# Moving loads between queues in a fused attention-and-FFN backward kernel: columns over GpSimd, a transposed operand in quarters, a written order for the output stage

## The chip, the core and the metric

The kernel is one launch on one core of a Trainium2 chip. A core has five instruction streams that run beside each other and meet at semaphores: TensorE (PE in the profile: matmuls out of SBUF into PSUM, with the weight loads PEld), VectorE (DVE), ScalarE (ACT), GpSimd (POOL) and SyncE (SP). Data moves between HBM and SBUF by DMAs, which one of SyncE, ScalarE and GpSimd issues from its own in-order stream; all of them share the core's 16 DMA engines. An instruction at the head of a stream that waits for a semaphore holds everything behind it in that stream, whether that is a DMA issue or a compute instruction.

The metric is the device time of the launch in microseconds. Before the change it is 803.75 us, the median of six runs between 796.22 and 813.41.

## What is computed

The reference is a block of linear attention and a SwiGLU FFN, each behind a LayerNorm and with a residual, on x of 2048 x 640 in bf16, and the gradients of its output with respect to x and the five weights, for a given grad_out:

```python
def _A_ref(x, wqkv, wo):                    # 32 heads of 20
    q, k, v = split(x @ wqkv)
    phi = lambda t: jnp.where(t > 0, t + 1, jnp.exp(t)) + 1e-6
    pq, pk = phi(q), phi(k)
    kv = jnp.einsum("bhsd,bhse->bhde", pk, v)
    z = jnp.einsum("bhsd->bhd", pk)
    num = jnp.einsum("bhqd,bhde->bhqe", pq, kv)
    den = jnp.einsum("bhqd,bhd->bhq", pq, z)[..., None] + 1e-6
    return merge_heads(num / den) @ wo
def _B_ref(x, w_gate, w_up, w_down):        # 640 -> 1728 -> 640
    return (_silu(x @ w_gate) * (x @ w_up)) @ w_down
h = x + _A_ref(_layernorm(x), A_wqkv, A_wo)
out = h + _B_ref(_layernorm(h), B_w_gate, B_w_up, B_w_down)
# returned: out, and the vjp of grad_out for x, wqkv, wo, w_gate, w_up, w_down
```

## The kernel before

The 2048 rows are 16 tiles of 128 rows (`ST = 16`), the 640 columns five blocks of 128 (`DT = 5`). PSUM holds four two-bank tiles at a time, all from one pool (`mm`). SBUF is parted into pools whose buffers are reused: five large ones, four "strips" (tag "S"), two pools of row tiles (`wk`), a ring of seven `fw` tiles, and three staging tiles "stg".

The stages in order of time: LayerNorm 1 with keys and queries (0 to 52 us); the attention forward; the FFN forward and its weight gradients in four groups `g` of 448, 448, 448 and 384 of the 1728 hidden columns (143 to 449 us); the gradient of the hidden activations, in eight pairs of row tiles (449 to about 570 us); the attention backward (to about 724 us); the output stage (to 800 us).

**The FFN groups.** For each group a loop over pairs of row tiles makes gate and up products (L796, L801), the activation on ScalarE (L817 to L823) and seven products on VectorE (L829). SyncE then transposes each tile of gradients by DMA into a staging tile and stores it to the scratch `scr_dT` (L832, L785). After the loop `dw_group` makes the group's weight gradients: plain products in `dw` (`ps_dw`, L881, copied out by `copy` at L883 on ScalarE or VectorE) alternate with a fast scheme of sums and products (`ps_wa`, `ps_wc`, L690; sums on VectorE, L686). In the last group (g = 3) VectorE also makes sums of the gate weights (`wg_tsum`, L658) and of the first columns (`col_sum`, L669).

**The columns.** The next stage reads the transposed gradients back in pairs of row tiles: `load_cols(p)` loads pair p from `scr_dT` in four DMAs, one for each group, into a strip. Pairs 0 and 1 are loaded on ScalarE's queue by `act_load`, which keeps the written order: pair 0 right before `dw_group` of group 3, pair 1 at its end. Pairs 2 to 7 go over GpSimd's queue (`pool_load`, where the scheduler picks the place). `pool_store` is a DMA on GpSimd's queue that keeps its written order against other such DMAs. On GpSimd's queue also stand the stores of all weight gradients, the loads `pq` for rows 13 to 15 (L641), which use the three staging tiles, and later the loads `pkr`.

[...]

**Around GT.** At the end of the backward pairs, `dp_1` and `dp_2` finish the gradient of the queries tile by tile: `dp_a` and `dp_b` on VectorE, two `widen` copies and the copies out of PSUM on ScalarE. TensorE meanwhile makes the five products `ps_gt` (L929), copied to `GT` by ScalarE (L1201 for the first, L1244 for the others). `xn_act` normalises rows of x on ScalarE, as filler for that stage. Then `xnT_r`, the transposed normalised x, is loaded in four quarters of 640 KB, all held until `last_pq`, the last load of `pq`, by `tc.issue_after`; SyncE at the same time transposes 16 pieces of `wqkv` (`wqkvT`), then pieces for `ring`, `wvk` and `ring` again. The loop that follows runs `t` over 19 steps: `ps_dk` of tile t (L110), and `ps_dxn` of tile t - 3 (L1364).

**The output stage.** out = h + FFN in seven pairs of row tiles by a fast scheme (`step_a` to `step_f`), with the tiles of h loaded over GpSimd's queue (`load_h1`, L1394) and most of the results stored there (`o_store`, L1479). `load_mT` is SyncE's transposing load of the hidden activations. TensorE and ScalarE keep the written order; GpSimd's order is the scheduler's.

Of the kernel before, what the change touches and what calls it, by code (L numbers as in the profile page):

```python
# [13 lines left out]
EngineType = mybir.EngineType  # L14
# [6 lines left out]
def kernel(  # L21
# [600 lines left out]
    with tc.manual_schedule(engines={EngineType.SP}):  # L622
# [48 lines left out]
        def dw_group(g, w, m_s, dd, dw, dwd_part, dgu_part):  # L671
# [95 lines left out]
            tt(ev[:, :, :w], pc[:, :, :w], u2, ALU.add)  # L767
            store(ev, 1, 0)
            if g == 3:
                load_cols(1, act_load)  # L770

        wgT = {}

# [13 lines left out]
        for g in range(4):  # L787
# [59 lines left out]
            if g == 0:  # L847
                wdT = strips.tile([P, DT, 2 * GM], BF16, name="wdT", tag="S")
                load_wdT(wdT, 2)
            elif g == 1:  # L850
                wgT[0] = big.tile([P, 16, D], BF16, name="wgT", tag="B")
                for gg in range(2):
                    tr_wgT(gg)
                    load_wgu(gg + 2)
            elif g == 2:
                dm_t[3] = strips.tile([P, ST, GM], BF16, name="dm3", tag="S")
                act_load(dm_t[3][:, :, :GW[3]], scr_dm_v)
                wgT[1] = big.tile([P, 16, D], BF16, name="wgT", tag="B")
                tr_wgT(2)
                tr_wgT(3)  # L860
            else:
                for c in range(4):
                    pool_store(scr_m_v[:, c * 4:(c + 1) * 4, F:FT * P], m_s[:, c * 4:(c + 1) * 4, w - 64:w])
                pool_store(mat_v(scr_dwdT)[:, 0:4, F:FT * P], zpad)
                pool_store(mat_v(scr_dwdT)[:, 4, F:FT * P], zpad[:, 0, :])
                load_cols(0, act_load)
                wsum = big.tile([P, ST * D], BF16, name="wsum", tag="B")
                for i in (1, 2):
                    wg_t[i] = wsum[:, (i - 1) * HKG * 320:i * HKG * 320].rearrange("p (k n) -> p k n", k=HKG)
                wg_t["S1"] = wsum[:, 2 * HKG * 320:2 * HKG * 320 + HKG * P].rearrange("p (k c) -> p k c", k=HKG)  # L870
# [61 lines left out]
    with tc.manual_schedule(engines={EngineType.PE, EngineType.DVE, EngineType.Activation, EngineType.SP, EngineType.Pool}):  # L932
# [49 lines left out]
        def load_q(t):  # L982
            if 0 <= t < ST:
                pqs[t] = small.tile([P, D], BF16, name="pq", tag="stg", bufs=3, padded_shape=[P, 7 * P])[:]
                return nc.gpsimd.dma_start(out=pqs[t], in_=scr_pq_v[:, t, :]).ins

        def dp_mm(t):
            if t >= 0:
# [178 lines left out]
        kb = [dqs[:, i * D:(i + 1) * D] for i in (8, 9, 10)]  # L1167
        prs, rxs = [kb[0], junk], kb[1:]

        def dp_1(t):  # L1170
            dp_a(t, prs[t % 2])
            widen(rxs[t % 2], rall, t)
            widen(prs[t % 2], nS1, t)

        def dp_2(t):
            last = dp_b(t, prs[t % 2], rxs[t % 2])
            return last, load_q(t + 3)

        dp_1(ST - 5)
        dp_mm(ST - 4)  # L1180
# [3 lines left out]
            gts[i] = mm("ps_gt")  # L1184
            gt_part(gts[i], i, 0, ST - 4, ST if i else 4)
        dp_mm(ST - 3)
        dp_1(ST - 3)
        last_pq = dp_2(ST - 4)[1]
        nc.gpsimd.dma_start(out=hn[:, ST - 4:ST, :], in_=x_v[:, ST - 4:ST, :])
        store_dwd(p - 1)  # L1190
        store_dwd(p)
        gts[2] = mm("ps_gt")
        gt_part(gts[2], 2, 0, ST - 4)
        dp_mm(ST - 2)
        xn_act(range(6, 9))
        dp_1(ST - 2)
        dp_2(ST - 3)
        GT = mat(2 * DT * D, DT, D)
        ps = gts.pop(0)
        gt_part(ps, 0, ST - 4, ST)  # L1200
        nc.scalar.copy(out=half(GT[:, 0, :]), in_=row(ps))  # L1201
        dp_mm(ST - 1)
        xn_act(range(9, 11))
        dp_1(ST - 1)
        dp_2(ST - 2)
        xn_act(range(11, ST - 4))
        last_dq = dp_2(ST - 1)[0]

    with tc.manual_schedule(engines={EngineType.SP, EngineType.DVE}):

# [18 lines left out]
        for k in (0, 1):  # L1229
            for i in range(DT):  # L1230
                with tc.issue_after(last_dh1T):
                    tr_piece(wqkvT[:, 5 * k:5 * k + 5, :], A_wqkv[:, k * D:(k + 1) * D], i)
        for c in range(4):
          with tc.issue_after(last_pq):
            pool_load(xnT_r[:, 4 * c:4 * c + 4], scr_xnT[4 * c:4 * c + 4].rearrange("t p k c -> p t k c"))

        for i in range(1, DT):
            ps = gts.pop(i, None)
# [81 lines left out]
        def load_mT(t):  # L1320
            if t % 4 == 0:
                mTs[t // 4] = strips.tile([P, 4, FT, P], BF16, name="mT", tag="S")
            nc.sync.dma_start_transpose(out=mTs[t // 4][:, t % 4], in_=scr_m[t * P:(t + 1) * P, :])

        for t in range(ST + LAG):
            if t in (2, 3):
                dwqk(0, t + 1)
            if t < ST:
                if t + 2 < ST:
                    load_pk(t + 2)  # L1330
                pkr = pkrs.pop(t)
                nc.vector.tensor_scalar(out=pkr[:], in0=pkr[:], scalar1=-1e-6, scalar2=1.0, op0=ALU.add, op1=ALU.min)
                tk = wk("tk", pool=1)
                ps = mm("ps_dk")
                mm_row(ps, lambda i: xnT_r[:, t, i, :], lambda i, n0, n1: WK2[:, i, n0:n1], DT)
                nc.vector.scalar_tensor_tensor(out=half(tk[:]), in0=row(ps), scalar=rstd1[:, t:t + 1] if t < NC else 1.0,
                                               in1=half(dzb[:]), op0=ALU.mult, op1=ALU.add)
                nc.vector.tensor_tensor(out=dk[:, t, :], in0=tk[:], in1=pkr[:], op=ALU.mult)
                nc.sync.dma_start_transpose(out=ring[:, t % 4], in_=dk[:, t, :])
                if t < 2:  # L1340
                    load_pqT(t + 1)
            if 8 <= t < 8 + HG:
                tr_cols(G[:, t - 8, :], scr_GT, OH[t - 8])
            if t == 14:
                nc.sync.dma_start_transpose(out=KV.rearrange("p j c -> p (j c)").unsqueeze(1), in_=scr_KVT)
            if t == ST:
                dKV = stage()[:, :HG, :]
                nc.sync.dma_start_transpose(out=dKV, in_=dKVT.rearrange("p j c -> p (j c)"))
            if t == ST:
                wd = big.tile([P, FT, D], BF16, name="wd", tag="B")  # L1350
                nc.sync.dma_start(out=wd[:, :13, :], in_=B_w_down[0:13 * P, :].rearrange("(j p) d -> p j d", p=P))
                for r in (0, 64):
                    nc.sync.dma_start(out=wd[r:r + 64, 13, :], in_=B_w_down[13 * P:F, :])
            u = t - LAG
            if u < 0:
                continue
            if t >= ST:
                dwqk(1, t - ST)
            pkT, dqT, dkT = ring[:, 4 + u % 3], ring[:, 7 + u % 3], ring[:, u % 4]
            ps = mm("ps_dxn")  # L1360
            for ci, (n0, n1) in enumerate(NCH):
                for k, (lhs, rhs) in enumerate(((dqT, wqkvT[:, 0:5]), (pkT, WV2), (dkT, wqkvT[:, 5:10]))):
                    for i in range(DT):
                        nc.tensor.matmul(ps[:, ci, :320], lhsT=lhs[:, i, :], rhs=rhs[:, i, n0:n1],  # L1364
                                         start=(k == 0 and i == 0), stop=(k == 2 and i == DT - 1))
            if u + 3 < ST:
                load_pqT(u + 3)
            if ST - MTA <= u:
                load_mT(u - ST + MTA)
            dx = wk("dx")  # L1370
            ln_bwd(ps, xn_r[:, u, :], rstd1[:, u:u + 1], dh1[:, u, :], dx[:], 0)
            nc.gpsimd.dma_start(out=o1_v[:, u, :], in_=dx[:])
# [10 lines left out]
        def dwv(i):  # L1383
# [2 lines left out]
            mm_heads(ps, lambda j: Y[:, j, i * P:(i + 1) * P], lambda j, a, b: dKV[:, j, a:b])  # L1386
            nc.scalar.copy(out=half(ev[:]), in_=row(ps))
            nc.sync.dma_start(out=out_2[i * P:(i + 1) * P, 2 * D:3 * D], in_=ev[:])

        h1rs = {}  # L1390

        def load_h1(t):
            h1rs[t] = wk("h1r", pool=t % 2)
            nc.gpsimd.dma_start(out=h1rs[t][:], in_=scr_h1_v[:, t, :])  # L1394

        NP = ST // 2 - 1
        HK = 6
# [97 lines left out]

        CH15 = [(0, 320), (320, 512), (512, 640)]

        with tc.manual_schedule(engines={EngineType.PE, EngineType.Activation}):
            for t in range(4):
                load_h1(t)  # L1500
            for t in (5, 6):
                load_mT(t)
# [16 lines left out]

            for p in range(NP):  # L1520
                v = p - 1
                load_h1(2 * p + 4) if 2 * p + 4 < ST else None
                load_h1(2 * p + 5) if 2 * p + 5 < ST else None
                for t in (2 * p + 7, 2 * p + 8):
                    if t < ST:
                        load_mT(t)
                for j in range(2 * p + 2, min(2 * p + 4, HG)):
                    tr_cols(Y[:, j, :], scr_Yt, OH[j])
                step_a(p)
                if v < 0:  # L1530
                    tt(T4, B21, T2)
                    next(fill)
                    step_b(p)
                    step_c(p)
                    osum(p + 1, 0)
                    osum(p + 1, 1)
                    next(fill)
                    next(fill)
                    tt(T5, BL[0], BL[1])
                    for k, i in ((0, 3), (1, 2), (1, 3)):  # L1540
                        osum(p + k, i)
                    continue
                step_d(v)
                step_b(p)
                c22(v)
                osum(p + 1, 0)
                step_c(p)
                step_e(v)
                osum(p + 1, 2)
                step_f(v)  # L1550
                osum(p + 1, 1)
                osum(p + 1, 3)
                if p not in (2, 3):
                    f, i = small_q.pop(0)
                    f(i)
# [63 lines left out]
```

## Time and profile before

The profiled execution took 801.75 us, of which 800.0 us are the span from its first to its last instruction.

| what | measured |
|---|---|
| median of six runs | 803.75 us |
| profiled execution, and its span | 801.75 us, 800.0 us |
| TensorE busy | 782.0 us, 98% of the span |
| VectorE, ScalarE, GpSimd busy | 72%, 41%, 28% |
| mean granted TensorE clock | 0.994 of full speed |
| PE busy in 410 to 430 us | 12.27 of 20 us, clock 0.83 |
| PE busy in 735 to 769 us, and 769 to 800 us | 32.05 of 34, and 26.56 of 31 us |
| column loads issued by ScalarE (8): issue of one; landing | 0.37 to 0.50 us; median 5.1 us |
| column loads issued by GpSimd (24): issue of one; landing | 0.71 to 0.73 us; median 5.2 us |

A line of the timeline gives start and length in us, the engine (with q: its DMA queue), the line of the source, the operation and its tiles, the number of instructions, and in brackets how long the engine was idle before and what ended it. A line of the waits names who waited for whom, the total, the number of times and the longest. Matmul ends in the timeline are modelled, so the pace of matmuls is read from start to start.

### The profile page before, as it was taken

What the parts mean: (1) busy time and instruction counts of PE and PEld (TensorE: products, weight loads), DVE (VectorE), ACT (ScalarE), POOL (GpSimd) and SP (SyncE); (2) the same over time, 40 slices, a digit from 0 to 9 for tenths busy, and PEclk for the clock granted to TensorE, in tenths of its full rate; (3) what the DMA queues carried; (4) which work ended last, traced back from release to release, by engine and by line L of the source; (5) the groups of instructions that cost most, each with busy time, mean ns of one, the idle gap of its engine ahead of it and who ended that gap; (6) DMA issues with size and microseconds to landing.
All of it is one profiled execution on the core that took longest, in us unless ns stands there. A gap on an engine that the chain in (4) does not pass through costs nothing.

```text
span 800.0 us, 13753 instructions
## 1 busy us (share of the span) xinstructions
PE 782.0 (98%) x5243; PEld 498.3 (62%) x5243; DVE 575.6 (72%) x1005; ACT 331.7 (41%) x490; POOL 221.3 (28%) x375
## 2 busy tenths in 40 slices
PE   9999999999999999999996999999999999999988
PEld 7676566555555555555653677777667677777655
DVE  7979988894697648747974777999882366626763
ACT  6972532760283145402810245676662133333001
POOL 4600047413301111144032253532431112114220
PEclk9999999999999999999997999999999999999999
DMA  9799999999979978999796789998999988899992
GB/s 259 157 240 307 197 225 251 262 266 235 225 187 225 216 172 202 251 252 229 175 211 190 202 245 232 186 231 200 191 223 205 162 173 169 174 256 245 189 237 75
DMA packets 295731, 170.62 MB, mean 213 GB/s; under 512 B 242780, under 2 KB 283741, under 8 KB 295664
## 3 DMA queue, kind: packets, MB, share of 16 engines
q1 hardware_dynamic: 271552, 102.84, 63.7%
q0 software_dynamic: 19584, 61.57, 27.8%
q10 hardware_dynamic: 4528, 5.33, 2.2%
q8 instruction: 41, 0.67, 0.4%
q14 instruction: 26, 0.21, 0.1%
HBM read 52.92 MB, written 56.28 MB: 136 GB/s over the span
## 4 chain that ended last, share of the span: by engine, by line
PE 84%; DVE 7%; DMA 5%; SPq 2%; issue 1%; ACT 1%; POOL 0%; ACTq 0%; DVEq 0%
PE ps_dw L881 9%; PE ps_dxn L1364 8%; PE ps_dhn L955 7%; PE ps_wa L690 7%; PE pg L796 6%; PE pu L801 6%; PE ps_dm L423 5%; PE ps_dhc L955 5%; PE ps_dwqk L1283 5%; PE ps_kq L311 4%; PE ps_wc L690 3%; PE ps_y L514 3%; PE ps_a L577 3%; PE ps_dk L110 2%; PE ps_oa L1434 2%; PE pdm L423 2%
## 5 line engine op out<-in xcount | busy, mean ns | idle before, releaser
L955 PEld LDWEIGHTS <-cols 128*128 128x128 bf16 x624 | 61.1, 98 | 23.7
L796 PE MATMUL pg<-wgu,hnT 128*128 128x448 bf16 (+1 forms) x320 | 63.6, 346 | 0.0
L801 PE MATMUL pu<-wgu,hnT 128*128 128x448 bf16 (+1 forms) x320 | 63.6, 346 | 0.0
L881 PE MATMUL ps_dw<-m_s,dh 128*128 128x448 bf16 (+1 forms) x320 | 60.7, 347 | 0.0
L1364 PEld LDWEIGHTS <-ring 128*128 128x128 bf16 x480 | 46.9, 98 | 19.6 <-DMA ring<-dk 1.5
L1364 PE MATMUL ps_dxn<-wqkvT,ring 128*128 128x320 bf16 x320 | 51.3, 299 | 1.2 <-DMA ring<-dk 1.2
L881 PEld LDWEIGHTS <-dh 128*128 128x128 bf16 x320 | 31.5, 98 | 27.5 <-issue 0.7
L801 PEld LDWEIGHTS <-hnT 128*128 128x128 bf16 x320 | 31.3, 98 | 27.1
L796 PEld LDWEIGHTS <-hnT 128*128 128x128 bf16 x320 | 31.3, 98 | 27.0
L423 PEld LDWEIGHTS <-dh2T 128*128 128x128 bf16 x320 | 31.0, 98 | 25.1
L423 PE MATMUL ps_dm<-wdT,dh2T 128*128 128x448 bf16 (+1 forms) x240 | 46.5, 344 | 0.0
L311 PE MATMUL ps_kq<-wqk,xnT 128*128 128x320 bf16 x320 | 45.3, 301 | 0.7 <-DMA xnT<-xn 0.7
L817 ACT ACTIVATE dd<-pg 128x896 bf16<-128x896 f32 (+1 forms) x32 | 28.5, 891 | 40.4 <-PE pg L796 36.0
L690 PEld LDWEIGHTS <-S 128*128 128x128 bf16 x256 | 25.7, 101 | 31.1 <-issue 10.4
L311 PEld LDWEIGHTS <-xnT 128*128 128x128 bf16 x320 | 31.1, 99 | 13.2 <-DMA xnT<-xn 1.0
L1283 PEld LDWEIGHTS <-hn 128*128 128x128 bf16 x320 | 31.0, 98 | 12.2 <-issue 0.3
L140 POOL TENSOR_SCALAR lnv<-mv 128x1 f32<-128x1 f32 x32 | 11.9, 373 | 90.8 <-DVE mv L136 73.9
L843 POOL DMA_DIRECT2D scr_m<-m_s x16 | 12.1, 757 | 88.7 <-DVE m_s L829 88.7
L148 DVE CUSTOM_DVE_ANT_0 lb_a<-lb_dy,hn 128x640 bf16<-128x640 bf16 x16 | 13.2, 825 | 31.7 <-ACT lb_dy L146 31.7
L690 PE MATMUL ps_wc<-dd,S 128*128 128x448 bf16 (+1 forms) x128 | 27.2, 370 | 7.7 <-ACT dwev L883 7.7
L686 DVE TENSOR_TENSOR dd<-dd 128x3584 bf16<-128x3584 bf16 (+1 forms) x12 | 23.1, 1953 | 13.4 <-PE ps_wa L690 13.4
L146 ACT ACTIVATE lb_dy<-ps_dxn,rstd 128x640 bf16<-128x640 f32 x16 | 12.7, 794 | 46.3 <-PE ps_dxn L1364 46.3
(259 smaller groups left out, 1781.5 us busy)
## 6 DMA issues: line engine op xcount, KB each, us to landing
scr_dT<-stg SPq DMA_DIRECT2D x48, 224.0 KB, 3.1
cols<-scr_dT POOLq DMA_DIRECT2D x18, 448.0 KB, 5.2
scr_m<-m_s POOLq DMA_DIRECT2D x12, 448.0 KB, 4.6
pq<-scr_pq POOLq DMA_DIRECT2D x32, 160.0 KB, 5.4
hn<-in_A_x_dram SPq DMA_DIRECT2D x5, 640.0 KB, 5.6
scr_dT<-stg SPq DMA_DIRECT2D x16, 192.0 KB, 3.1
cols<-scr_dT ACTq DMA_DIRECT2D x6, 448.0 KB, 5.1
scr_pq<-pqa SPq DMA_DIRECT2D x4, 640.0 KB, 4.7
```

Source lines behind the costliest of these rows:

```text
L311: nc.tensor.matmul(ps[:, ci, :320], lhsT=xnT[:, t, k, :], rhs=wqk[:, k, w0 + n0:w0 + n1], start=(k == 0), stop=(k == DT - 1))
L423: nc.tensor.matmul(ps[:, c, :w], lhsT=dh2T[:, kt, (t + c) * P:(t + c + 1) * P], rhs=wdT[:, kt, o:o + w], start=(kt == 0), stop=(kt == DT - 1))
L514: nc.tensor.matmul(ps[:, ci, :320], lhsT=xn[:, t, i * P:(i + 1) * P], rhs=pk[:, t, n0:n1], start=(t == 0), stop=(t == ST - 1))
L577: nc.tensor.matmul(ps[:, ci, :320], lhsT=pqsT[:, i, t * P:(t + 1) * P], rhs=W2[:, i, n0:n1], start=(i == 0), stop=(i == DT - 1))
L690: nc.tensor.matmul(out, lhsT=lhs[:, t, :], rhs=rhs[:, t, :], start=(first and t == 0), stop=(t == 7), skip_group_check=not first)
L796: nc.tensor.matmul(pg[:, c, :w], lhsT=hnT[:, kt, (t + c) * P:(t + c + 1) * P], rhs=wg[:, kt, 0:w], start=(kt == 0), stop=(kt == DT - 1))
L801: nc.tensor.matmul(pu[:, c, :w], lhsT=hnT[:, kt, (t + c) * P:(t + c + 1) * P], rhs=wg[:, kt, w:2 * w], start=(kt == 0), stop=(kt == DT - 1))
L817: sig = nc.scalar.activation(out=dg, in_=pg[:, :, :w], func=ACT.Sigmoid)
L881: nc.tensor.matmul(ps[:, c, :w], lhsT=lhs(t), rhs=rhs(t), start=(t == 0), stop=(t == ST - 1))
L955: nc.tensor.matmul(out, lhsT=lhs[:, k, :], rhs=rhs[:, k, :], start=(first and k == 0), stop=(k == HKG - 1), skip_group_check=not first)
L1283: nc.tensor.matmul(ps[:, ci, :320], lhsT=xn_r[:, t, i * P:(i + 1) * P], rhs=dq[t // 8][:, t % 8, n0:n1] if which == 0 else dk[:, t, n0:n1] ...
L1364: nc.tensor.matmul(ps[:, ci, :320], lhsT=lhs[:, i, :], rhs=rhs[:, i, n0:n1], start=(k == 0 and i == 0), stop=(k == 2 and i == DT - 1))
```

## The change

Four things, here cut to their core:

```diff
@@ dw_group, and the loop over groups
             if g == 3:
-                load_cols(1, act_load)
+                load_cols(1, pool_store)
...
-                load_cols(0, act_load)
+                load_cols(0, pool_store)
@@ around GT
-        def dp_1(t):
+        def dp_1(t, ts=()):
             dp_a(t, prs[t % 2])
             widen(rxs[t % 2], rall, t)
+            xn_act(ts)
             widen(prs[t % 2], nS1, t)
...
         dp_mm(ST - 3)
-        dp_1(ST - 3)
-        last_pq = dp_2(ST - 4)[1]
+        dp_1(ST - 3, range(6, 8))
+        dp_2(ST - 4)
...
         dp_mm(ST - 2)
-        xn_act(range(6, 9))
-        dp_1(ST - 2)
+        dp_a(ST - 2, prs[0])
+        xn_act(range(8, 9))
         dp_2(ST - 3)
         GT = mat(2 * DT * D, DT, D)
         ps = gts.pop(0)
         gt_part(ps, 0, ST - 4, ST)
         nc.scalar.copy(out=half(GT[:, 0, :]), in_=row(ps))
+        widen(rxs[0], rall, ST - 2)
+        widen(prs[0], nS1, ST - 2)
         dp_mm(ST - 1)
-        xn_act(range(9, 11))
-        dp_1(ST - 1)
+        dp_a(ST - 1, prs[1])
         dp_2(ST - 2)
-        xn_act(range(11, ST - 4))
-        last_dq = dp_2(ST - 1)[0]
+        widen(rxs[1], rall, ST - 1)
+        widen(prs[1], nS1, ST - 1)
+        xn_act(range(9, ST - 4))
+        last_dq = dp_2(ST - 1)
@@ transposed x
-        for c in range(4):
-          with tc.issue_after(last_pq):
-            pool_load(xnT_r[:, 4 * c:4 * c + 4], scr_xnT[...])
+        def load_xnT(c):
+            pool_store(xnT_r[:, 4 * c:4 * c + 4], scr_xnT[...])
+
+        load_xnT(0)
+        load_xnT(1)
@@ the loop over t
         for t in range(ST + LAG):
+            if t >= ST:
+                for i in ((0,), (1, 2), (3,))[t - ST]:
+                    load_h1(i)
...
                 if t + 2 < ST:
                     load_pk(t + 2)
+                if t in (2, 6):
+                    load_xnT(2 + t // 6)
@@ output stage
-        with tc.manual_schedule(engines={EngineType.PE, EngineType.Activation}):
-            for t in range(4):
+        with tc.manual_schedule(engines={EngineType.PE, EngineType.Activation, EngineType.Pool}):
+            for t in (4, 5):
                 load_h1(t)
...
             for p in range(NP):
-                load_h1(2 * p + 4) if 2 * p + 4 < ST else None
-                load_h1(2 * p + 5) if 2 * p + 5 < ST else None
+                for t in (2 * p + 4, 2 * p + 5):
+                    if p > 0 and t < ST:
+                        load_h1(t)
```

In the built program this moves the following. The eight loads of pairs 0 and 1 leave ScalarE's stream. Pair 0's stand on GpSimd's behind the last two zero stores to `scr_dwdT`; pair 1's behind the last stores of group 3 from `m_s`, and so behind the three `pq` loads and eleven stores that follow them. On GpSimd's queue the two first `pkr` loads now come before the first two quarters of `xnT_r`; the third quarter stands behind the fifth `pkr` load, the fourth behind the ninth. On ScalarE the first GT copy comes before the two widening copies of row tile 14, and the normalising copies move behind it or into the preceding steps. The first four loads of h are issued from the last three steps of the loop over t, and in the output stage each pair's two loads stand between the stores of the results two pairs before. The numbers of matmuls, VectorE instructions and DMAs, and all their sizes, stay as they were.

More of the change, by code (lines that the diff above doesn't have):

```diff
@@ L984, in load_q @@
                 pqs[t] = small.tile([P, D], BF16, name="pq", tag="stg", bufs=3, padded_shape=[P, 7 * P])[:]
-                return nc.gpsimd.dma_start(out=pqs[t], in_=scr_pq_v[:, t, :]).ins
+                nc.gpsimd.dma_start(out=pqs[t], in_=scr_pq_v[:, t, :])
         def dp_mm(t):
@@ L1176, in dp_2 @@
             last = dp_b(t, prs[t % 2], rxs[t % 2])
-            return last, load_q(t + 3)
+            load_q(t + 3)
+            return last
         dp_1(ST - 5)
@@ L1232 @@
                     tr_piece(wqkvT[:, 5 * k:5 * k + 5, :], A_wqkv[:, k * D:(k + 1) * D], i)
-        for c in range(4):
-          with tc.issue_after(last_pq):
-            pool_load(xnT_r[:, 4 * c:4 * c + 4], scr_xnT[4 * c:4 * c + 4].rearrange("t p k c -> p t k c"))
+        def load_xnT(c):
+            pool_store(xnT_r[:, 4 * c:4 * c + 4], scr_xnT[4 * c:4 * c + 4].rearrange("t p k c -> p t k c"))
+        load_xnT(0)
+        load_xnT(1)
         for i in range(1, DT):
@@ L1323, in load_mT, with load_h1 @@
             nc.sync.dma_start_transpose(out=mTs[t // 4][:, t % 4], in_=scr_m[t * P:(t + 1) * P, :])
+        h1rs = {}
+        def load_h1(t):
+            h1rs[t] = wk("h1r", pool=t % 2)
+            nc.gpsimd.dma_start(out=h1rs[t][:], in_=scr_h1_v[:, t, :])
         for t in range(ST + LAG):
+            if t >= ST:
+                for i in ((0,), (1, 2), (3,))[t - ST]:
+                    load_h1(i)
             if t in (2, 3):
@@ L1388, in dwv @@
             nc.sync.dma_start(out=out_2[i * P:(i + 1) * P, 2 * D:3 * D], in_=ev[:])
[L1390 to L1394, printed above, removed]
         NP = ST // 2 - 1
```

## The prediction

> **What bounds the kernel now.** I read first the busy shares, then TensorE's own waits, then the chain of waits where the longest lies, then the timeline and a windows table there.
>
> ```profile
> PE 782.0 (98%) x5243; PEld 498.3 (62%) x5243; DVE 575.6 (72%) x1005; ACT 331.7 (41%) x490; POOL 221.3 (28%) x375
> ```
>
> TensorE is the bound: an edit elsewhere counts only where TensorE stands still or runs at a lower clock. Its waits (line; who ended them; us in total, times, longest) leave few such places:
>
> ```profile
> PE ps_wc L690 <- ACT dwev L883: 7.7, 1, 7.7
> PE ps_oa L1434 <- DVE h1r L1418: 2.5, 1, 2.5
> PE ps_dxn L1364 <- DMA ring<-dk: 1.2, 1, 1.2
> ...
> PE ps_gt L929 <- ACT mats L1201: 0.4, 1, 0.4
> ```
>
> Each lies in a place that the diff touches. The chain (start, length, what) shows what is behind the first:
>
> ```profile
> 411.03 8.88 DMA scr_dT<-stg
> ...
> 419.93 1.21 SPq L832
> 421.14 0.04 issue
> 421.19 0.61 SPq L785
> ...
> 421.89 5.09 DMA stg<-dd
> 426.99 0.79 ACT dwev L883
> 427.78 0.04 issue
> 427.82 5.28 PE ps_wc L690 x16
> ```
>
> A transpose on SyncE ends ScalarE's wait, and ScalarE's copy, of 0.8 us, ends TensorE's. The timeline tells what ScalarE did meanwhile:
>
> ```profile
> 411.11 15.76 ACTq L159 DMA_DIRECT2D cols<-scr_dT  x4
> 417.33 2.76 PE L881 MATMUL ps_dw<-m_s,dh 128*128 128x384 bf16 x16
> ...
> 426.97 0.80 ACT L883 CAST dwev<-ps_dw 128x768 bf16<-128x768 f32 x1 [23.76 <-DMA stg<-dd]
> ```
>
> ScalarE stood idle for 23.76 us with pair 0's four loads at its head, while the copy behind them could have run at 417.33 + 2.76 = 420.09. The windows table (stretch, length, busy time of PE, PEld, DVE, ACT, POOL; then the granted clock, DMA share, GB/s) shows the aftermath:
>
> ```profile
> 419.90:427.80 7.90, 0.19 (x2) 0.00 (x0) 0.00 (x0) 0.83 (x2) 0.00 (x0) 0.72 0.92 240
> 427.80:433.10 5.30, 5.28 (x17) 2.46 (x17) 3.15 (x5) 0.73 (x2) 1.09 (x2) 0.50 0.70 212
> 433.10:438.50 5.40, 5.40 (x33) 3.18 (x32) 5.26 (x4) 0.00 (x0) 3.21 (x6) 0.96 0.45 152
> ```
>
> After the gap TensorE makes 16 products in 5.3 us at half clock.
>
> **Part 1, pair 0 off ScalarE: -10.7 us.** The neighbouring block of 32 matmuls of 384 columns takes 438.44 - 433.24, about 5.20 us from start to start, 0.1625 us each. The 16 products `ps_wc` after the gap took 432.89 - 427.82 = 5.07 us where 16 x 0.1625 = 2.60 are due, so 2.47 are lost. The next 32 took 438.44 - 432.89 = 5.55 for 5.20: 0.35 lost. The gap itself is 427.82 - 419.93 = 7.89. Sum 7.89 + 2.47 + 0.35 = 10.71 us, if the copy is on time.
>
> [...]
>
> What is late next? From 419.93 to the end of the group TensorE has 112 such matmuls, 18.2 us, so the next stage starts at T0 = 438.13 instead of 448.83. VectorE has 16.1 us of work in that stretch by its rows. Its tightest step, an addition read out of the product `ps_wc`, would be done at 434.6 and is needed at 435.5: slack 0.9. Groups 0 to 2, with no loads on ScalarE, show no wait of TensorE at this place. That is why I take the whole 10.7; the low end is zero, if another wait takes over.
>
> [...] By the rows, the clock is 0.50 for the first 5.3 us after a wait of 7.7, and 1.00 after those of 2.5 and 1.2 (windows from 769.5 and 631.6). [...]
>
> **Part 1, pair 1: 0 to +3.3, taken +0.5.** Its four loads now queue on GpSimd behind the three `pq` loads, which wait for staging buffers until SyncE's last stores are done: the last is issued at 433.31 + 0.54 = 433.85 in the trace, and SyncE's pace does not change. Behind them come eleven stores, 0.535 us each: nine end at 433.85 + 4.8 = 438.66. The other two wait for VectorE's last sum at T0 + 1.17 = 439.3 and end at 440.66. Pair 1 is issued from 440.66 to 443.5, so T0 + 2.5 to T0 + 5.4; before it was issued 2.3 to 0.3 us ahead of T0. Needed: two quarters at T0 + 9.1 = 447.2, VectorE's sum at 448.5, the others at 450.9. With 5.2 us landing the last comes at 448.7 and the first two by 447.3: no cost to a few tenths. With 9.1, the longest landing of ScalarE's loads under SyncE's traffic, 3.3 us late. By 438 SyncE has drained and the DMA share is at 0.22 to 0.45, so the value is near the lower end; +0.5. If SyncE's drain moved the last `pq` issue beyond some 434.8, each us would come through almost whole.
>
> [...] The rows: 0.37 to 0.50 us an issue on ScalarE and 0.71 to 0.73 on GpSimd, so 8 x 0.3 = 2.4 us more issue time, on an engine at 28%; landing 5.1 and 5.2. [...]
>
> **Part 2, quarters of x: -1.15, between 0 and +2.** TensorE's 1.15 us wait at 630.4 is for the transpose of `dk` of tile 0, issued by SyncE only at 628.16 though its data were ready at 617.8; SyncE was late since ten transposes of `wqkvT` took 29.08 us from 589.42, beside 2.62 MB of transposed x. Two quarters out of that stretch are 1.31 MB, at the measured 222 GB/s 5.9 us of traffic. SyncE needs to be only 1.15 us earlier. The first two quarters go behind the second `pkr` load, issued at 592.34: issued by 594.4, landing by 594.4 + 12.6 (longest before) = 607, needed at 614.8. The third stands behind the fifth `pkr` load (623.55), landing by 637, needed about 656; the fourth behind the ninth (650.21), 664, needed about 678. The price on the upside: the third quarter's traffic beside the 1.2 us ring transposes, which run with little slack at 624 to 636.
>
> **Part 3, GT copy: -0.4.** TensorE's 0.43 wait goes, since the copy now precedes two widening copies and the fillers. The moved fillers (two rows, 1.74 us) fit ahead of tile 13's second widening copy. The last copies of the queries' gradient end at 594.8 and are needed at 598.2 less a margin: 1.9 us of slack covers the shifts of 0.7 or less. Without that cover, up to 0.7 is lost.
>
> **Part 4, output stage: 0, between -2.5 and +2.5.** The 2.46 us wait at 769.5 is ended by VectorE, but VectorE itself stood 3.88 us for SyncE's transposing load of the hidden activations, at a DMA share of 1.19. That load is not touched. Of h, six tiles instead of five are issued before 731, and 14 by 760 either way; a pair is issued some 14 us before use and lands in 7.7 (median) to 10.0 (longest). GpSimd's fixed order binds h loads to stores of results from two pairs before, whose data are ready by then. So no gain and no loss; the bounds are the wait removed, and as much again.
>
> **Sum.** 800.0 - 10.7 - 1.15 - 0.4 + 0.5 = 788.2 span, about 790 profiled with the 1.75 us outside the span. The profiled run is 2.0 below the median of six, so the median becomes 803.75 x 788.2/800 = 791.9: 792 us.
>
> **Rivals and chances.** About 1% (8 us) is what a measurement can tell from no change.
>
> A, the forecast, 0.62: 789 to 795, all but the small terms holding.
>
> B, 0.17: the gap closes but pair 1 comes late, or SyncE's drain holds GpSimd: 2 to 6 us back, 794 to 799. For it: eleven stores and three waiting loads ahead. Against it: nine of these have 0.535 us rows and no wait.
>
> C, 0.10: another wait takes the gap's place. Pair 0's loads might meet a wait on GpSimd as long as ScalarE's, with the stores of `dwev` behind them; the buffer then is late for the copy, and TensorE stands again. Or VectorE's slack of 0.9 fails. A gap of 2.5 us leaves the clock, by the rows; one of 7.7 halves it and brings back the 2.8. 798 to 805. Against: GpSimd's data dependences are tiles 0 and 1 alone.
>
> D, slower, 0.11: the fixed GpSimd order in the output stage. Each pair's loads of h would wait for a store that waits for VectorE's result, and TensorE then for h. It breaks even with the gains when seven pairs lose 11.8 us together, 1.7 each; to be 8 us slower they lose 2.8 each, a landing of 14 + 2.8 = 17 us where 10.0 is the longest seen: 806 to 820. For it: GpSimd waited 4.35 and 5.80 us before loads of h at 759.8 and 767.2 already. Against: none of these reached TensorE.
>
> The range of 786.5 to 801 takes in A, B and most of C, with a margin below for the six runs' own scatter; it leaves out D and C's end. Below 795.7 (faster) lie all of A and a third of B: 0.68. Above 811.8 (slower) lies most of D: 0.08. Same: 0.24.
>
> **What would show it.** Right: no wait of TensorE at `ps_wc` in group 3 and a clock of 1.00 between 410 and 440; ScalarE's idle time before that copy under a few us; the next stage starting near 438. `ps_dxn` without a wait for `ring<-dk`; no wait at `ps_gt` for L1201. Wrong: a wait of TensorE or VectorE for `cols` between 445 and 455 (B); a wait before `ps_wc` of another releaser (C); waits for `h1r` that end in a DMA of h, or GpSimd idle before its loads of h beyond 5.8 us (D).

## The result, and the profile after

The changed kernel takes 796.14 us, median of 28 runs (787.33 to 811.23), beside 803.9 us for the kernel before (63 runs, 793.29 to 817.79). The ratio is 0.9916, 95% interval 0.9889 to 0.9942: 6.8 us faster, where 11.75 were forecast. It lies in the range, but the likeliest case (A, 789 to 795, given 0.62) isn't what happened: 796.14 lies in that of B (794 to 799, given 0.17), and the sign named for B, a wait for `cols` between 445 and 455, is there. Both kernels scatter by some 3%, and the ratio leaves each kernel's longest runs out; the profiled execution of the changed kernel, 801.72 us, is one of these, so its waits are the ones that make such a run long; that its span is 800.0 us like that of before is chance.

TensorE's waits in it (same columns as before):

```profile
PE ps_dhn L955 <- DMA cols<-scr_dT: 8.4, 2, 7.0
PE ps_dhc L955 <- DMA cols<-scr_dT: 3.1, 1, 3.1
PE ps_warm L347 <- DVE ones L249: 1.1, 1, 1.1
```

All four waits that the prediction spoke of are gone, and 11.5 us of waits for columns stand in their place. The windows of the changed kernel (columns as before) show both ends of the exchange:

```profile
419.00:437.20 18.20, 18.20 (x114) 10.96 (x112) 15.49 (x15) 2.88 (x6) 1.09 (x2) 1.00 0.87 179
437.20:446.50 9.30, 9.26 (x68) 6.46 (x66) 6.02 (x7) 1.05 (x2) 5.99 (x12) 1.00 0.68 225
446.50:453.47 6.97, 0.00 (x0) 0.00 (x1) 0.55 (x1) 0.53 (x1) 6.09 (x9) 0.70 1.04 211
453.47:461.00 7.53, 6.16 (x28) 3.48 (x29) 0.00 (x0) 0.53 (x1) 0.00 (x0) 0.60 0.99 188
...
465.15:471.46 6.31, 6.31 (x35) 3.98 (x36) 5.84 (x9) 0.92 (x1) 0.99 (x2) 0.73 0.37 85
```

From `ps_wc` to the next stage TensorE now works through, 18.20 us at full clock, where 28.90 were needed: 10.70 won, to the hundredth what was worked out. Then it does pair 0 in 9.3 us, stands 7 us at the first product of pair 1, and goes on at a lowered clock, 0.60, and 0.73 behind a later wait of 3.1 us. The chain of waits names the way there:

```profile
438.69 0.53 POOL pq L641
439.22 0.54 POOL out_dram L696
...
446.38 0.54 POOL out_dram L696
446.92 1.56 POOL cols L165 x3
448.48 0.57 issue
449.05 16.05 DMA cols<-scr_dT
465.11 0.05 issue
465.15 0.99 PE ps_dhc L955 x6
```

GpSimd stays at the `pq` loads until 439, reaches pair 1's first load 7.7 us later, behind the stores, and pair 1's last load is then 16 us under way. GpSimd's timeline (in brackets: idle before, what ended it) shows what holds it, and what follows pair 1 at once:

```profile
434.74 0.54 POOL L641 DMA_DIRECT2D pq<-scr_pq  x1 [18.28 <-DMA scr_dT<-stg]
436.54 0.54 POOL L641 DMA_DIRECT2D pq<-scr_pq  x1 [1.26 <-DMA scr_dT<-stg]
438.68 0.54 POOL L641 DMA_DIRECT2D pq<-scr_pq  x1 [1.60 <-DMA scr_dT<-stg]
...
446.91 2.85 POOL L165 DMA_DIRECT2D cols<-scr_dT  x4
450.14 2.82 POOL L162 DMA_DIRECT2D cols<-scr_dT  x4 [0.37 <-issue]
```

Two landmarks on TensorE measure this from here on: the start of the next stage (first `ps_dhn`, called T0) and the first `ps_dp`. Their lines before and then in the changed kernel:

```profile
448.83 1.93 PE L955 MATMUL ps_dhn<-wgT,cols 128*128 128x320 bf16 x13
483.74 1.52 PE L110 MATMUL ps_dp<-mats,dh1T 128*128 128x320 bf16 x10
...
437.20 1.93 PE L955 MATMUL ps_dhn<-wgT,cols 128*128 128x320 bf16 x13
488.03 1.52 PE L110 MATMUL ps_dp<-mats,dh1T 128*128 128x320 bf16 x10
```

Before they are 34.91 us apart, without a wait between them; in the changed kernel 50.83. So 11.6 us are won up to T0, 15.9 lost in the next stage, and the rest of the kernel, 316.3 us before and 312.0 after, wins 4.3.

Theories: *late second pair*, the loads stand too far back in GpSimd's queue; *crowded DMA* or *collision*, they land late because of what is under way beside them. *SyncE's drain* is the end of its transposes and stores of group 3, which the `pq` loads wait for.

### The profile page after: what moved, and what is told of

It reads as the page before. It is cut to its first block, busy times and chain, and to the rows that moved or that the text cites. A ratio compares the mean times of both kernels' runs of the same rounds, so it can differ in the third digit from the quotient of the medians.

```text
span 800.0 us, 13749 instructions
## 1 busy us (share of the span) xinstructions
PE 782.2 (98%) x5243; PEld 498.3 (62%) x5243; DVE 575.5 (72%) x1005; ACT 331.7 (41%) x490; POOL 226.9 (28%) x383
## 3 DMA queue, kind: packets, MB, share of 16 engines
q10 hardware_dynamic: 2352, 1.79, 0.8%
## 4 chain that ended last, share of the span: by engine, by line
PE 89%; DVE 4%; DMA 3%; issue 1%; POOL 1%; ACT 1%; SPq 0%; POOLq 0%; ACTq 0%; DVEq 0%
PE ps_dw L881 10%; PE ps_dxn L1382 8%; PE pg L796 7%; PE pu L801 7%; PE ps_wa L690 6%; PE ps_dhn L955 6%; PE ps_dwqk L1290 5%; PE ps_dm L423 5%; PE ps_dhc L955 5%; PE ps_kq L311 4%; PE ps_oa L1446 4%; PE ps_dk L110 3%; PE ps_y L514 3%; PE ps_a L577 3%; PE ps_wc L690 3%; DMA cols<-scr_dT 2%
## 5 line engine op out<-in xcount | busy, mean ns | idle before, releaser
L955 PE MATMUL ps_dhn<-wgT,cols 128*128 128x320 bf16 x208 | 32.7, 310 | 8.4 <-DMA cols<-scr_dT 8.4
L311 PEld LDWEIGHTS <-xnT 128*128 128x128 bf16 x320 | 30.9, 98 | 12.7 <-DMA xnT<-xn 0.7
L977 POOL DMA_DIRECT2D dh<-lb_a x16 | 14.5, 909 | 74.6 <-DVE lb_a L976 51.0
L955 PE MATMUL ps_dhc<-wgT,cols 128*128 128x320 bf16 x208 | 32.3, 308 | 3.1 <-DMA cols<-scr_dT 3.1
```

The source lines that it names most:

```text
L311: nc.tensor.matmul(ps[:, ci, :320], lhsT=xnT[:, t, k, :], rhs=wqk[:, k, w0 + n0:w0 + n1], start=(k == 0), stop=(k == DT - 1))
L955: nc.tensor.matmul(out, lhsT=lhs[:, k, :], rhs=rhs[:, k, :], start=(first and k == 0), stop=(k == HKG - 1), skip_group_check=not first)
```

## The experiments

**Once more the changed kernel.** No edit.

> The changed kernel once more, to see whether its long profile is typical. Landmarks on TensorE: the next stage starts (first ps_dhn), and the first ps_dp. Before: 448.83 and 483.74, 34.91 apart; changed kernel: 437.20 and 488.03, 50.83 apart. Theory 'late second pair': the 15.9 us between are the price of pair 1's columns, and the spread of the runs (787 to 811) is how late they land. So a profile with a span near 788 shows the stage at 437 to 438, 35 to 38 us apart and under 2 us of waits for cols; one near 800 shows some 50 and 10 or more of waits. Rival 'clock only': the spread has nothing to do with pair 1; a span near 788 has waits for cols as long as one near 800, and the clock is lower elsewhere.

Measured: 799.73 us, ratio 0.9905 (0.9866 to 0.9944); over all 40 runs of the changed kernel the median is 797.1. This time the profile is of a short execution, span 788.3. T0 is 437.21, the landmarks are 38.24 apart, and the waits for columns are 1.9 us (a wait for ScalarE's `lb_a` behind them adds 0.8):

```profile
PE ps_dhn L955 <- DMA cols<-scr_dT: 1.0, 2, 0.7
PE ps_dhc L955 <- DMA cols<-scr_dT: 0.9, 1, 0.9
```

GpSimd's timeline of this execution:

```profile
434.31 0.54 POOL L641 DMA_DIRECT2D pq<-scr_pq  x1 [1.36 <-DMA scr_dT<-stg]
...
442.55 0.73 POOL L165 DMA_DIRECT2D cols<-scr_dT  x1
444.31 2.14 POOL L165 DMA_DIRECT2D cols<-scr_dT  x3 [1.03 <-DMA scr_dwdT<-dwev]
446.44 2.83 POOL L162 DMA_DIRECT2D cols<-scr_dT  x4
```

The last `pq` load is issued 4.4 us sooner, and pair 1 with it. T0 is equal to 0.01 us in both profiles; the 12.6 us between the landmarks are more than the 11.7 between the spans. "Clock only" falls for this pair of profiles.

**Pair 1 back on ScalarE.**

```diff
-                load_cols(1, pool_store)
+                load_cols(1, act_load)
```

> The changed kernel with pair 1's four loads back on ScalarE; pair 0's stay on GpSimd. 'Late second pair' (they wait on GpSimd behind three pq loads and eleven stores): the stage starts at 437 to 438, the landmarks are 35 to 36 us apart, no wait for cols over 1 us, span 784 to 787, ratio to before 0.978 to 0.983. Rival 'crowded DMA' (pair 0's burst at 410 slows SyncE's drain, and whatever is loaded around 437 lands late): ScalarE's loads wait for SyncE's DMAs too and land late, waits for cols of 5 to 10 us stay, span 794 to 800, ratio 0.99 or more.

Measured: 787.63 us, ratio 0.984 (0.9789 to 0.9892), span 783.5. T0 is 436.81, the landmarks are 34.91 us apart as before the change, with no wait for columns. ScalarE's line:

```profile
434.57 2.06 ACTq L159 DMA_DIRECT2D cols<-scr_dT  x4
```

And the landing of these loads (KB each, median us to landing):

```profile
cols<-scr_dT ACTq DMA_DIRECT2D x3, 448.0 KB, 4.3
cols<-scr_dT ACTq DMA_DIRECT2D x1, 384.0 KB, 8.8
```

The loads are issued from 2.2 us ahead of T0 instead of from 5 to 10 behind it. "Crowded DMA" as a whole falls for this execution: with pair 0's burst in place, nothing is late.

**The same again.** No further edit.

> Once more the changed kernel with pair 1 on ScalarE (its first six runs: median 787.6, ratio 0.984). If it is the better version: ratio 0.978 to 0.988 again, landmarks 34.9 to 36 us apart, no wait for cols. If the first six were a lucky draw from the spread of the changed kernel: median 795 to 800, ratio 0.99.

Measured: 788.19 us, ratio 0.9883 (0.9816 to 0.9949), span 784.8, landmarks 34.91 apart. Over the 12 runs of both the median is 788.1; four are above 795, of the changed kernel's 40 it is 25. By the medians this version beats both kernels, by some 9 us the changed one; the intervals of the ratios overlap with that of the changed kernel, so the size of that is open.

**Part 1 alone,** on the kernel before: both pairs by `pool_store`, the two lines of part 1 in the diff.

> The kernel before with only part 1 (both pairs' loads on GpSimd). 'Late second pair': the stage starts near 438, then 36 to 51 us to the first ps_dp; without the three other parts the time is 2 to 4 us above that of the changed kernel in the same rounds: ratio to before 0.993 to 1.000. The prediction's own sum for this part, -10.2 us, would be 0.987.

Measured: 799.66 us, ratio 0.9931 (0.9889 to 0.9972). T0 is 437.32, the landmarks are 38.99 apart with 2.8 us of waits for columns. The profile is of a very long execution (span 814.6), in which another load is the late one:

```profile
PE ps_dp L110 <- DMA dh1T<-dh: 12.7, 1, 12.7
```

`dh1T` is one of SyncE's transposes. Between 437 and 500 us these landed in 16.6 us (median) here, in 7.2 with pair 1 on ScalarE. So the late landings reached beyond the columns. What set it off wasn't found.

**Pair 0 alone,** on the kernel before: only `load_cols(0, ...)` by `pool_store`.

> The kernel before with pair 0 alone on GpSimd. By the prediction's first term -10.7 us: ratio 0.987. With pair 1 on ScalarE no wait for cols, stage at 437 to 438, 35 to 36 us between the landmarks. Rival 'given back': DVE or SyncE takes the gap's place, stage later than 441, ratio over 0.993.

Measured: 797.29 us, ratio 0.9891 (0.9814 to 0.9967), span 787.6, T0 437.07, the landmarks 34.91 apart. The span's gain is 12.4 us and the ratio's 8.8: the first term of the sum is in keeping with both, within a wide interval, and isn't given back.

**Parts 2 to 4 alone:** the changed kernel with both pairs by `act_load`.

> The changed kernel with both pairs' loads back on ScalarE: parts 2 to 4 alone. The wait of 7 to 8 us at ps_wc and the half clock are back. By the prediction's terms -1.6 us: ratio 0.998. By the two profiles (from the first ps_dp to the end 316.3 us before, 312.0 after) -4.3 us: ratio 0.995, with no TensorE wait at ps_oa.

Measured: 799.72 us, ratio 0.9994 (0.996 to 1.0028): -0.5 us, with -1.6 forecast and both inside the interval. The wait at `ps_wc` is back with 6.2 us. The waits at `ps_gt` are gone and that at `ps_oa` is 0.3, but `ps_dxn` still waits 1.5.

**Pair 1 on GpSimd, but ahead** of the `pq` loads and the last four stores.

```diff
+            if g == 3:
+                load_cols(1, pool_store)
+                pq_load(range(13, ST), False)
             late = m_s[:, 12:16, :].rearrange("p (k u) n -> p k u n", k=2)
...
-            if g == 3:
-                load_cols(1, pool_store)
...
-            if p == 0:
-                pq_load(range(13, ST), False, nc.gpsimd.dma_start)
```

> The changed kernel, pair 1's loads still on GpSimd, but written ahead of the three pq loads and of the last four stores. 'Late in the queue': the loads are issued at 432 to 435, land before 447, TensorE waits for cols under 1 us, 35 to 36 us between the landmarks, ratio to before as with pair 1 on ScalarE, 0.980 to 0.988. Rival 'GpSimd's queue lands slower, wherever it stands': waits of 1 to 10 us for cols remain, 38 to 51 us between the landmarks, ratio 0.990 to 0.995 as for the changed kernel.

Measured: 797.62 us, ratio 0.9899 (0.9834 to 0.9965), span 789.9. The loads are issued at 437.12, later than hoped but 5 to 10 us sooner than in the changed kernel; they land in 8.3 and 9.4 us, and no wait for columns is left. But the stores went out sooner too; SyncE's queue, which waits for them, moved up, its transposes of `wo` now start at 440.08 instead of 446 to 447, and TensorE waits 3.2 us for `dh1T`: the landmarks are 38.25 apart. In this profile the waits for columns went with the place in the queue, not with the queue; the time is between both theories.

**Only the `pq` loads behind pair 1.**

```diff
                 load_cols(1, pool_store)
+                pq_load(range(13, ST), False)
...
-            if p == 0:
-                pq_load(range(13, ST), False, nc.gpsimd.dma_start)
```

> The changed kernel with only the three pq loads put behind pair 1's loads on GpSimd; all stores stay ahead. If the pq loads' wait for SyncE's drain is what makes pair 1 late: the loads are issued at 438 to 442 in every execution, waits for cols under 2 us, median 786 to 792, ratio 0.980 to 0.988. If the eleven stores and their semaphores hold GpSimd as long: issued at 442 to 447, waits of 1 to 10 us, ratio 0.990 or more.

Measured: 794.62 us, ratio 0.9942 (0.9898 to 0.9986), span 792.9. Pair 1 is issued at 440.04, as the first theory wanted, and yet TensorE waits 2.7 us for columns, in pieces of 1.9 and 0.9, and goes on at half clock: its next six products take 1.58 us from start to start, in the short execution above 0.83; the landmarks are 39.38 apart. The landing:

```profile
cols<-scr_dT POOLq DMA_DIRECT2D x3, 448.0 KB, 9.7
cols<-scr_dT POOLq DMA_DIRECT2D x1, 384.0 KB, 10.8
```

SyncE's transposes of `wo` are issued from 439.60 in this version, in the same microseconds. A sooner issue alone isn't enough: a miss for "late in the queue" as the whole cause.

**The transposes of `wo` out of the way.** SyncE issues three of them right behind the load of `W2T`, at 438.33 to 444.1.

```diff
         woT = mat(DT * D, DT, D)
+        for i in range(3):
+            tr_piece(woT, A_wo, i)
...
-        WO_AT = {0: (0, 1, 2), 6: (3,), 7: (4,)}
+        WO_AT = {6: (3,), 7: (4,)}
```

> The changed kernel with SyncE's three transposes of wo issued right behind the load of W2T near 438 instead of at 446 to 452; pairs 1 and 2 stay back to back on GpSimd. 'Collision' (pairs 1 and 2 together with these transposes land in 8 to 20 us, where either alone takes 4 to 9): pair 1 lands in 4 to 8 us, waits for cols of 2 us or less in every profile, transposes landing in under 8 us, runs above 800 disappear, median 787 to 790, ratio 0.980 to 0.986. Rival 'late in the queue alone': pair 1 is issued as late as before and its waits stay (2 to 11 us), median 795 to 800, ratio 0.990 or more.

Measured: 796.98 us, ratio 0.9942 (0.9903 to 0.998), span 801.4. SyncE's drain is as late here as in the changed kernel's profile (last `pq` load at 438.65, there 438.68), so the two compare well. Pair 1 is issued even later, from 449.63, and lands in half the time:

```profile
cols<-scr_dT POOLq DMA_DIRECT2D x3, 448.0 KB, 4.9
cols<-scr_dT POOLq DMA_DIRECT2D x1, 384.0 KB, 5.8
```

In the changed kernel it was

```profile
cols<-scr_dT POOLq DMA_DIRECT2D x3, 448.0 KB, 9.2
cols<-scr_dT POOLq DMA_DIRECT2D x1, 384.0 KB, 16.1
```

Pair 2 follows at once in both, so in these two profiles pair 1 landed sooner for want of the transposes, not of pair 2. The wait for columns is 6.5 us in one piece instead of 11.5 in three, the landmarks are 43.64 apart instead of 50.83. So lateness alone costs 8.7 here, and the 7.2 more in the changed kernel go to the collision, as far as one profile of each can tell. My number for the time was wrong: without the collision, lateness stays.

**Both remedies:** pair 1 on ScalarE and the transposes of `wo` early.

> Pair 1 on ScalarE and the transposes of wo early, as an attempt at the best version. 'Collision' was gone already with pair 1 on ScalarE: no difference from that version, 784 to 788, ratio 0.978 to 0.985. If the early transposes now meet ScalarE's loads of pair 1 (issued from 434.6): waits for cols of 1 to 5 us, ratio 0.985 to 0.992.

Measured: 786.67 us, ratio 0.9856 (0.9803 to 0.9909): no difference from pair 1 on ScalarE. Without the late issue there is no collision to remove.

**Part 4 undone,** with pair 1 on ScalarE: the hunks of the output stage taken back.

> Pair 1 on ScalarE, part 4 (GpSimd's order in the output stage, early loads of h) undone. The prediction's term for part 4 was 0, between -2.5 and +2.5. If part 4 removes the wait at ps_oa (2.5 before; 0.3, 0.7 and none in three kernels with part 4, but 5.2 and 4.6 in two others): ps_oa waits of 2 to 3 us, time 2 us above the version with part 4. If these waits are a matter of how the transposed hidden activations land in a given execution: anything from 0 to 5 us, and a ratio within 0.004 of that version's.

Measured: 788.67 us, ratio 0.9889 (0.9832 to 0.9947), equal to the version with part 4. The wait at `ps_oa` is 0.8 us, although the old order is back. Over all profiles that wait is 0 to 2.7 without part 4 and 0 to 5.2 with it.

**Part 2 undone,** with pair 1 on ScalarE: the four loads of transposed x held until `last_pq` as before.

> Pair 1 on ScalarE, part 2 (transposed x in quarters when due) undone. The prediction's term for part 2 was -1.15 us: the wait of ps_dxn for ring<-dk comes back with 1 to 4 us (1.2 before, 3.1 and 3.7 in two kernels without part 2, but 1.5 in one with it), time 1 to 4 us above the version with part 2. Rival 'no effect': no wait, or as much as with part 2.

Measured: 796.78 us, ratio 0.9916 (0.9857 to 0.9975), not told apart from the version with part 2 by the intervals. Of these 12 runs seven are above 795, of the 24 of the four versions with pair 1 on ScalarE and part 2 it is six: a hint, no more, that part 2 is worth more than its wait. The wait is back, now put down to `ring<-dq`, 1.1 us. Here SyncE's drain was late too (last `pq` load at 440.09), yet ScalarE had issued pair 1 at 437.75, and there is no wait for pair 1's columns: ScalarE's queue didn't wait here for the end of that drain. The landmarks are 38.65 apart all the same, with waits of 0.7 us for pair 2's columns, 0.8 for a sum of columns on VectorE and 1.7 for `pq`. So with this late drain the stage loses 3.7 us even with pair 1 on ScalarE, and of the 8.6 us that this span is longer than that with part 2 (792.1 against 783.5) only 1.7 lie behind the first `ps_dp`, where part 2 acts.

## Why the prediction was right, and where it was wrong

**Pair 0, -10.7: right.** T0 - 419.00 is 18.20 us, and the landmarks with pair 0 alone lie as close as before. VectorE and SyncE, named as what could be late next, took nothing back. One reading behind the term was off and did no harm: the 433.24 behind the pace of 32 matmuls isn't the start of a block; the block from 438.44 to 443.63 gives 5.19 us for 5.20. Before, ScalarE issued pair 0's loads at 411.11, 419.93, 421.02 and 426.50, each within 0.1 us of the landing of a transpose or a store of SyncE's. In the changed kernel's profile GpSimd issues them from 410.52 to 413.35 without a pause, ending 14.8 us before the transpose that SyncE issued at 411.05 lands. They landed in 8.9 us (448 KB) and 13.9 (384 KB), where GpSimd's column loads before took 5.2 (median); pair 0 was there by about 427 and VectorE first reads it at 434.82, so this cost nothing.

**Pair 1, "0 to +3.3, taken +0.5": the term that was mis-sized.** The way was named (case B), but it costs 3.3 us (38.24 - 34.91) in a short execution and 15.9 in a long one. That 3.3 equals the upper bound is luck: counted like the 5.2, from the end of the second issue, a landing of 9.1 us would have given 4.0. Three things in its working failed. "SyncE's pace does not change": the last `pq` load came at 434.31 in one execution, 438.68 in the other, for 433.31. The eleven stores and the loads: first load 7.7 us after the last `pq` in both profiles, 6.8 forecast, and in the short execution then a 1.03 us pause in the middle of pair 1, ended by an earlier store. That an earlier store of GpSimd's own could hold one of these loads was not in the working. And "the value is near the lower end" took the landing from loads with little beside them and a DMA share of 0.22 to 0.45, where the windows above have 0.68 and then 1.04; the transposes of `wo`, which SyncE issues at 446 to 455, were not in the working at all. The bounds should have reached from 5.2 to the landing of loads under transposes, and from there past the waiting time to the clock: "each us would come through almost whole" left out the half clock.

**The half clock.** It is in the rival C of the prediction, but B was priced without it. In the long execution 15.9 - 11.5 = 4.4 us are left beside the waits, most of it in two episodes of half clock behind waits of 7.0 and 3.1 us; with `wo` early it is 8.7 - 6.5 = 2.2, in one. By start to start an episode costs 1.4 us (only the `pq` loads behind), 1.6 (pair 1 ahead), 2.8 (before) or 2.9 (part 1 alone, `ps_dxn`). That a gap of 2.5 us leaves the clock, on which C's price rests, doesn't hold in every profile. The same ten products `ps_dxn` with pair 0 alone and with part 1 alone:

```profile
621.99 1.53 PE L1364 MATMUL ps_dxn<-wqkvT,ring 128*128 128x320 bf16 x10 [3.73 <-DMA ring<-dk]
...
641.42 2.85 PE L1364 MATMUL ps_dxn<-wqkvT,ring 128*128 128x320 bf16 x10 [3.09 <-DMA ring<-dk]
```

Behind the longer wait the ten took 1.53 us, in an execution with a mean granted clock of 1.00; behind the shorter 2.85. At `ps_oa` a wait of 2.46 us before the change left 12 products at 1.79 us, one of 2.50 with only the `pq` loads behind made them 3.30. Each of the five waits above 6 us (6.2, 6.5, 7.0, 7.7 and 12.7) was followed by products at a lowered pace: behind the 6.2 the 16 `ps_wc` took 3.91 us from start to start for 2.60, behind the 12.7 the ten `ps_dp` 2.64 for 1.36. From 2.5 to 3.7 us it went both ways, and what decides there is open.

**The two queues.** Pair 1 landed in 4.3 and 8.8 us from ScalarE and in 4.9 and 5.8 from GpSimd once the transposes were gone. The landing by queue didn't decide; what stands ahead in the queue, and what the loads then meet, did.

**Part 2, -1.15: direction right, size open.** All four profiles of kernels without it have a wait of 1.1 to 3.7 us at `ps_dxn` for `ring` (before, part 1 alone, pair 0 alone, part 2 undone); of the ten with it, one has (1.5). No run separates it in time.

**Part 3, -0.4: right.** The wait of `ps_gt` for ScalarE is 0.4 to 0.6 us in the three profiled kernels without it (before, part 1 alone, pair 0 alone), none in the others.

**Part 4, 0 within 2.5: right for the time, with a too narrow bound on its wait.** The `ps_oa` wait goes to 5.2 us in one profile with part 4, and it comes and goes with either order. In the two profiles where it is longest, 5.2 and 4.8 us, VectorE waits 12.4 and 11.6 us for `mT`, the transposing load of the hidden activations, which the prediction had named as left untouched; elsewhere that is 0 to 5.2.

**Rival D** didn't occur: no wait for a load of h in any profile with part 4.

**Open:** why SyncE's drain is 4 to 6 us late in some executions, and why pair 1 on ScalarE still has runs up to 806 us; no profile of such a run was taken. In the changed kernel's profile the lateness is one transpose, issued at 411.05 beside pair 0's four loads on GpSimd: it lands after 17.1 us, and SyncE waits 8.2 us in one piece for it. In the short execution the one at this place lands after 10.4. So pair 0's burst is not cleared of slowing the drain in the long executions.

## What to carry to other kernels

When loads move to another queue, list what stands ahead of them there up to the last waiting instruction, and price the landing with the traffic of the time at which they will be issued, not of that at which they were. A load that blocks an engine and one that doesn't can be separated: here only pair 0's had to move. Where a kernel scatters by 3%, one profile is one draw; two landmarks on the bounding engine, one on each side of the changed stage, tell what the totals can't.

## What the runs showed that was not expected

In the changed kernel's profile SyncE's transposes of `wo` and GpSimd's loads of pair 1 took 1.9 to 3.3 times as long to land as in the profiles that kept them apart, and two pairs of columns were under way at once. In four profiles (pair 1 on ScalarE twice, part 4 undone, pair 0 alone) the three transposes of `wo` ran beside pair 2's four loads alone and landed in 6.0 to 6.9 us (median), pair 2's loads of 448 KB in 5.5 to 6.5. Beside pairs 1 and 2 on GpSimd the transposes took 15 to 20 us. With pair 1 on ScalarE, and in the changed kernel:

```profile
mats<-in_A_wo_dram SPq DMA_TRANSPOSE x3, 6.0
...
mats<-in_A_wo_dram SPq DMA_TRANSPOSE x3, 20.0
```

Pair 1 took 9.2 and 16.1 us in the changed kernel, against 4.9 and 5.8 with the transposes out of the way. The bytes moved meanwhile stayed at 188 to 257 GB/s, in the changed kernel's windows from 446.5 to 465.15.
